# Attention outputs in any of eight PSUM banks, masked products in half-bank pieces on GpSimd, and buffers kept for the open unit

## The chip, the cores and the metric

The kernel runs on one core of a Trainium2 chip. The metric is the device time of one execution in microseconds. The engines of the core are TensorE (PE: matrix products; PEld is its loading of weights), VectorE (DVE), ScalarE (ACT), GpSimd (POOL) and SyncE (SP, which here issues nearly all transfers). PSUM is the memory that TensorE writes; this kernel uses it as eight banks of 128 x 512 float32.

## The reference

One layer mixes an attention block (32 heads of 16, 2048 rows, width 512) with a gated feed-forward network of width 1792:

```python
x = A_x                                            # 1 x 2048 x 512, bf16
g = sigmoid((x * gate_w).sum(-1, keepdims=True))
q, k, v = split(x @ wqkv)                          # 32 heads of 16
p = softmax(einsum("bhqd,bhkd->bhqk", q, k) * 16 ** -0.5)
a = einsum("bhqk,bhkd->bhqd", p, v) @ wo
b = (silu(x @ w_gate) * (x @ w_up)) @ w_down
return g * a + (1 - g) * b
```

The bulk is the softmax: 32 heads x 2048 x 2048 scores, each of which needs an exponential.

## The kernel before

**Units and tiles.** The queries are cut into four blocks of 512 (`QB`), the heads into eight groups of four (`G`). A *unit* is one block and one group, so there are 32. A unit goes over 16 *key tiles* of 128 keys; a key tile has four scores (one per head), each 128 keys x 512 queries, that is one PSUM bank. There are 512 key tiles, 2048 banks of scores.

**Two ways to an exponential.** Most key tiles go to ScalarE: `emit_group` (L913) writes two or three scores side by side as row tiles of TensorE (`score`, L819), and one `Exp` activation reads the banks and writes `e_all` (L255 is the line of every activation, L252 that of every matrix product, L267 that of every instruction of VectorE, GpSimd and SyncE, as helpers record them). The rest, called *masked scores* in this text, go to VectorE: `emit_d` (L1001) lets one or two scores ride in the same row slot, and VectorE turns a bank into 16-bit integers `y` (`c_t`, in one of `NS` = 7 buffers, `take_home`, `home`) whose bits, read as bf16, are a piecewise linear power of two. The curve is mended in one of two ways, chosen per tile by `quad` (L1807):

- a *four-copy tile*: `y` itself and three copies with other integers added (`SHIFTS`) are summed by TensorE, so the tile costs four products with V. Two of the copies are made by VectorE at full width (`copy`, L1104). The third is the *lift*: GpSimd adds the integer (as 32-bit pairs, one bank of `y` is 256 elements) in pieces of one or more banks (`lifted`, L1045).
- a *two-copy tile*: VectorE masks out the mantissa bits and the exponent bits (`bits`, L1113), multiplies `y` by the first mask (`product`, L1122), and TensorE sums product and second mask, two products with V.

**Products with V.** `pv` (L1224) writes four column tiles of 128 x 32 weights that run side by side; over a unit they add up in one bank. That bank is a tile of its own pool, `ps_o`, with one buffer. When a unit is through, `close` (L1647) has VectorE evict the bank (`post`, L1283); `o_ready` (L1654) lets the first product of the next unit start once the eviction is planned to be over. The seven other banks (`NP` = 7, the tile `psum`) go round between scores, masked scores and everything else.

**Side work.** The projections of x to q, k and v, the feed-forward network, the normalisation and the output products are cut into pieces (`columns`, L550) that a `Pacer` releases slot by slot; `side` picks one when TensorE has room before ScalarE's next group is due.

**Order.** The whole order is written out at build time by a planner that keeps estimated clocks for TensorE, VectorE, ScalarE and GpSimd (`plan`), a list of when each bank comes free (`banks`), and constants (L123 to L152) for its choices: how many scores to emit (`choose`, L852), whether another tile goes to VectorE (`v_unit`, L1782), whether it becomes a two-copy tile. `beside` (L1082) puts a lift piece next to reads of PSUM by VectorE, because VectorE's copies from buffer to buffer and GpSimd get in each other's way: a lift waits for the last such copy (`fast_last`), and its size is what fits the reads that follow. Where VectorE has nothing else to do, it makes the rest of the lift itself (`own_now`, L1143).

Each recorded instruction depends on its bank's last user (`ordered`, L217).

Of the kernel before, what the change touches and what calls it, by code (L numbers as in the profile page):

```python
# [80 lines left out]
def kernel(  # L81
# [12 lines left out]
    nc = tc.nc  # L94
# [22 lines left out]
    EB = 9  # L117
    NE = 22
    NP = 7
# [13 lines left out]
    HUNGRY = 0.107  # L133
    KEEP = 2
    FED = 6.808
    W3 = -0.964
    N1 = 6
    N2 = 0.964
    LOW = 1.12
    EXTRA = 1.481  # L140
    NEXT = 1.017
    BURST = 8.876
    SHORT = 17
    BACK = 3
    FIRST = 0.087
    W3T = 0.087
    LATEST = 0.64
# [3 lines left out]
    SPARE = 0.253  # L151

# [12 lines left out]
    ps_o = ctx.enter_context(tc.tile_pool(name="ps_o", bufs=1, space=bass.MemoryType.PSUM))  # L165
# [207 lines left out]
    lift = const.tile([P, 2], U16, name="lift")  # L373
    nc.gpsimd.memset(lift[:], int(SHIFTS[2]))
# [28 lines left out]
    POOL_IN, POOL_FIX, POOL_ONE, POOL_PE, POOL_OVER = 0.12, 0.09, 0.45, 0.2, 0.1  # L403
# [440 lines left out]
    def horizon():  # L844
        return max(plan.act + dur(exps[-1][2]), exps[-1][0] + ACT_IN + ACT_COL * exps[-1][2]) if exps else plan.act
# [6 lines left out]
    def choose():  # L852

        late = max(plan.pe, horizon() - LATEST)
        want = wants()
        fed = thirst()
        side_b = int(side_bank())
        most = min(3, 4 * (hi[au] - at_) - quarter) if au == UNITS - 1 else 3
        hunger = max(0.0, min(1.0, (FED - fed) / FED))

        def left_over(used):
            ok = [b is not None and i not in used for i, b in enumerate(banks)]
            return sum(all(ok[i:i + 3]) for i in range(NP - 2)) + sum(all(ok[i:i + 2]) for i in range(NP - 1))

        def place(w, n, by):
            here = None
            for i, _ in runs(w, by):
                rel = max(banks[i:i + w])
                now = max(late, rel)
                for j, _ in (runs(n, now) if n else [(None, 1)]):  # L870
                    if n and (j < i + w and i < j + n):
                        continue
                    used = [*range(i, i + w), *(range(j, j + n) if n else ())]
                    if n and side_b and not any(b is not None and b <= now and k not in used for k, b in enumerate(banks)):
                        continue
                    got = max([rel] + [banks[k] for k in used])
                    mark = (max(got, plan.pe), -left_over(used), -max(banks[k] for k in used))
                    if here is None or mark < here[0]:
                        here = mark, list(range(i, i + w)), list(range(j, j + n)) if n else [], got
            return here and here[1:]  # L880
        best = None
        for w in range(2, most + 1) if most > 1 else (1,):
            fit = len(fitting(w))
            for n in range(min(want, 2) + 1):
                if n > fit and (fed >= LOW or n > 2):
                    continue
                p = place(w, n, late)
                if p is None:
                    continue
                free = NP - w - sum(b is None for b in banks) - sum(b is not None and b > late for b in banks)  # L890
                value = (W3 + W3T * min(fed, 4.0)) * (w - 2) + hunger * (0.0, N1, N2)[n] - EXTRA * (n > fit) + NEXT * min(free - n, 3)
                if best is None or value > best[0]:
                    best = (value, *p)
        if best:
            return best[1:]
        for w in range(min(2, most), 0, -1):
            p = place(w, 0, 1e9)
            if p:
                return p

    def next_banks(w):

        r, a, t, q = [], au, at_, quarter
        while len(r) < w and a < UNITS:
            r.append(4 * (a * KT + t) + q)
# [7 lines left out]
    def emit_group(s, ds, rel):  # L913
        nonlocal quarter, at_, begun
        w = len(s)
# [8 lines left out]
        e0 = e_run(w)  # L924
        e_next[0] = e0 + w
        k0, step = s[0], s[1] - s[0] if w > 1 else 1
        s_t = psum[:, k0:k0 + (w - 1) * step + 1:step, :]
# [5 lines left out]
        for k, b in enumerate(bs):  # L933
            score(psum[:, s[k], :], b, 32 if riders or w != 2 else 64)
            e_of[b] = e_all[:, e0 + k, :]
            e_slot[b] = e0 + k
# [6 lines left out]
        def exp():  # L943
            act(out=e_all[:, e0:e0 + w, :], in_=s_t, func=ACT.Exp, scale=inv_sqrt_dh)
            plan.act = max(plan.act + ACT_FIX, ready + ACT_IN) + ACT_COL * w
            for i in s:
                banks[i] = plan.act + ACT_PE
            for b in bs:
                e_end[b] = plan.act + ACT_PE
        exps.append((ready, exp, w))  # L950
# [40 lines left out]

    def home(i=None, t=0.0):
# [8 lines left out]
    def emit_d(ks, at_banks, rows=32):  # L1001
        if not vcur:
            n = v_take()
            waiting[n] = [NV, None, take_home()]
            vcur.update(n=n, left=list(range(NV)), y=None)
# [11 lines left out]
        def first():  # L1017
# [8 lines left out]
            if groups[n] == 4 and GPS:  # L1026
                if n not in jobs:
                    jobs[n] = [h, y, None, None, [], 0]
# [4 lines left out]
            if groups[n] == 2:  # L1033
                vops.extend([(0.6, lambda: bits(n, 0, y), ("y", n), n, True), (0.6, lambda: bits(n, 1, y), None, n, True),
                             (MUL_US, lambda: product(n, h, y), None, n, False)])
            else:
                users[h][0] = 2 + GPS
                ready(n, 0, h, y)
                for k in range(1, 4 - GPS):
                    vops.append((0.6, lambda k=k: copy(n, k, h, y), ("y", n) if k == 1 else None, n, True))  # L1040
# [4 lines left out]
    def lifted(n, m=1, own=False):  # L1045

        job = jobs[n]
        h, y, a, c, left, done = job
        if c is None:
            a, t = take_home()  # L1050
            c = job[3] = home(a, 0.0)[1]
# [6 lines left out]
        k = next(i for i in left if all(j in left for j in range(i, i + m)))  # L1058
        cols = slice(k * QBW, (k + m) * QBW)
        if own:  # L1060
            spend_v(0.07 + 0.1335 * m, 0.0, None, True)
            vec.tensor_scalar(out=c[:, cols], in0=y[:, cols], scalar1=SHIFTS[2], scalar2=None, op0=ALU.add)
            fast_last[0] = last_of[vec.engine.engine]
        else:
            ins = gps.tensor_tensor(out=c[:, cols].bitcast(I32), in0=y[:, cols].bitcast(I32),
                                    in1=lift[:, :].bitcast(I32).broadcast_to([P, m * QBW // 2]), op=ALU.add)
# [8 lines left out]
        if job[5] == NV:  # L1075
            jobs.pop(n)
            copies[n, 3] = (c.bitcast(BF16), a)
            vready.append((end, n, 3))
            drop(h, end)
            y_live[0] -= 1  # L1080

    def beside(span):  # L1082

        if not jobs or plan.pool > plan.dve + 0.05:
            return
        n = next(iter(jobs))
        left = sorted(jobs[n][4])
        if not left or jobs[n][3] is None and min(c_free) > plan.dve:
            return
# [14 lines left out]
    def copy(n, k, i, y):  # L1104
        h, c = home()
        vec.tensor_scalar(out=c, in0=y, scalar1=SHIFTS[k - 1], scalar2=None, op0=ALU.add)
        ready(n, k, h, c)
        if k == 3 - GPS:
            drop(i, plan.dve + 0.05)
            if not GPS:  # L1110
                y_live[0] -= 1

    def bits(n, k, y):  # L1113
        h, c = home()
# [14 lines left out]
    def c_ready():  # L1129
        return min(c_free) if not vops or vops[0][4] else 0.0  # L1130
# [6 lines left out]
    def pay_v():  # L1137
        cost, f, key, _, _ = vops.pop(0)
# [4 lines left out]
    def own_now(now):  # L1143

        if not jobs:
            return False
        n = next(iter(jobs))
        left = sorted(jobs[n][4])
        if not left or len(left) + jobs[n][5] < NV or jobs[n][3] is None and min(c_free) > now:
# [74 lines left out]
    def pv(n, k=None, most=QBW):  # L1224
# [12 lines left out]
        o = o_of[un]  # L1237
        first = pvs[un] in ((0, KT // 2) if un == 0 else (0,))
# [44 lines left out]
    def post(un):  # L1283
        qb, g = UNIT[un]
        osbs[un] = osb0[qb] if g == 0 else work.tile([P, QBW], BF16, tag="osb", name="osb")
        if un == 0:
            assert part_scaled
            vec.scalar_tensor_tensor(out=osbs[un][:, :], in0=o_of.pop(un)[:, :], scalar=tiny[:, 0:1], in1=o_part, op0=ALU.add, op1=ALU.add)
        elif un == UNITS - 1:
            act(out=osbs[un][:, :], in_=o_of.pop(un)[:, :], func=ACT.Identity, bias=tiny[:, 0:1], scale=1.0)  # L1290
        else:
            vec.tensor_scalar(out=osbs[un][:, :], in0=o_of.pop(un)[:, :], scalar1=tiny[:, 0:1], scalar2=None, op0=ALU.add)
# [79 lines left out]
    def tail(n):  # L1372

        for _ in range(n):
            tq, i = rest.pop(0)
            if tq == 3 and i == 0:
                a_ps.append(ps_o.tile([P, QBW], F32, tag="o", name="al_o"))
# [21 lines left out]
    warm = ps_o.tile([P, QBW], F32, tag="o", name="warm")  # L1399
# [56 lines left out]
    m_free(qp0, plan.pe + 2.0)  # L1456
    for g in (3, 4):
# [196 lines left out]
    def o_ready(now):  # L1654
        return closed in o_of or now is None or not closed or closed - 1 in osbs and o_end[0] <= now
# [35 lines left out]
    def begin(n):  # L1691
        plan.slot = n
        for c in need.get(n, []):
# [54 lines left out]
    def next_pv():  # L1748
        flush_act()
        while not pv_list(None):  # L1750
# [6 lines left out]
            elif jobs and jobs[next(iter(jobs))][4]:  # L1757
                lifted(next(iter(jobs)))
# [23 lines left out]
    def v_unit():  # L1782

        nonlocal vu
        if y_live[0] >= NY or min(c_free) >= 1e9 or sum(v[0] for v in vops) > 4.9 or (au, at_) < (0, 2):
# [186 lines left out]
```

## Time and profile before

| | us |
|---|---|
| median of 3 runs (763.38 to 765.28) | 763.42 |
| the profiled execution, its own time | 765.53 |
| its span, first to last instruction | 763.8 |
| PE busy / DVE busy | 744.7 / 718.6 |
| ACT busy / POOL busy | 744.6 / 192.3 |

Of the groups of instructions these matter as well: products with V in the row `o_ps<-e_all,vaug` (2012 instructions, 167.2 us) and `o_ps<-c_t,vaug` (1864, 142.0), scores in `psum<-qx,kaug` (1632, 253.7), the tanh of the gate in `th<-psum` (56, 34.4), the eviction of a unit's output in `osb<-o_ps,tiny` (30, 22.3, mean 744 ns).

How to read it: busy time counts a moment once per engine, however many instructions overlap in it, so four column tiles of 385 ns that run side by side count little more than one. A row gives how many instructions there are, their busy time, the mean of one, then the idle time of the engine just before them and what ended it. The chain of waits follows back from the last instruction to what released each one. In the view by stage each row is a stretch of the span with the busy time of every engine, the granted clock of TensorE, and the share and rate of the transfers.

### The profile page before, as it was taken

The numbers are of one execution on the slowest core, as the hardware profiler recorded it, in microseconds if no ns is written. First come the engines' busy times: TensorE is split into PE (matmuls) and PEld (weight loads), VectorE is DVE, ScalarE is ACT, GpSimd is POOL, SyncE is SP. The second block draws the span as 40 slices with busy tenths as digits, with TensorE's granted clock in tenths as the row PEclk, the third lists the DMA queues.
The fourth block names the chain that finished last, engine by engine and source line by source line (L and its number), as shares of the span: only waits on it lengthen the run. The fifth ranks groups of instructions, "written<-read, shape, count | busy, mean of one in ns | idle before, by whom it ended". The sixth has DMA issues, their size and how long they took to land.

```text
span 763.8 us, 24745 instructions
## 1 busy us (share of the span) xinstructions
PE 744.7 (98%) x10201; PEld 241.6 (32%) x10201; DVE 718.6 (94%) x1190; ACT 744.6 (97%) x835; POOL 192.3 (25%) x312
## 2 busy tenths in 40 slices
PE   8999999999999998999999999999999999999997
PEld 3333333333233332333233333333333333333232
DVE  6799999999999999899999999999999999999994
ACT  5999999999999999999999999999999999999996
POOL 5231120120433013334321113334212034131130
PEclk9999999999999999999999999999999999999999
DMA  9000212254210013121200041311000232100001
GB/s 220 10 2 15 50 33 47 52 135 89 62 28 10 17 44 77 31 62 30 50 13 18 23 103 35 76 34 44 8 23 19 68 79 45 44 19 12 15 30 36
DMA packets 91033, 34.57 MB, mean 45 GB/s; under 512 B 75488, under 2 KB 90472, under 8 KB 90920
## 3 DMA queue, kind: packets, MB, share of 16 engines
q1 hardware_dynamic: 89192, 32.66, 18.1%
q8 instruction: 80, 1.31, 0.7%
q10 hardware_dynamic: 1728, 0.33, 0.2%
q14 instruction: 33, 0.27, 0.1%
HBM read 21.55 MB, written 2.35 MB: 31 GB/s over the span
## 4 chain that ended last, share of the span: by engine, by line
PE 51%; ACT 29%; DVE 13%; issue 6%; DMA 1%; DVEq 0%; ACTq 0%
PE psum L252 34%; ACT e_all L255 27%; PE o_ps L252 16%; DVE c_t L267 7%; DVE kaug L267 2%; DVE mt L267 1%; DVE gs L267 1%; ACT th L255 1%; PE warm L252 1%; DVE osb L267 0%; DMA wg<-in_B_w_gate_dram 0%; DVE rd L267 0%; DMA out_dram<-o_t 0%; DVE o_t L267 0%; PE al_o L252 0%
## 5 line engine op out<-in xcount | busy, mean ns | idle before, releaser
L255 ACT ACTIVATE e_all<-psum 128x1024 bf16<-128x1024 f32 x766 | 716.7, 1044 | 4.0 <-PE psum L252 2.4
L267 DVE TENSOR_SCALAR c_t<-psum 128x512 uint16<-128x512 f32 x440 | 292.6, 683 | 16.3 <-PE psum L252 14.8
L252 PE MATMUL psum<-qx,kaug 32*128 32x512 bf16 (+1 forms) x1632 | 253.7, 385 | 8.1 <-ACT e_all L255 5.2
L267 POOL TENSOR_TENSOR c_t<-c_t,lift 128x256 int32<-128x256 int32 (+2 forms) x218 | 137.7, 637 | 427.2 <-DVE c_t L267 337.3
L252 PE MATMUL o_ps<-e_all,vaug 128*32 128x512 bf16 (+3 forms) x2012 | 167.2, 333 | 0.0
L252 PEld LDWEIGHTS <-kaug 32*128 32x128 bf16 (+1 forms) x2048 | 76.4, 91 | 273.1 <-ACT e_all L255 188.2
L252 PE MATMUL o_ps<-c_t,vaug 128*32 128x512 bf16 (+3 forms) x1864 | 142.0, 337 | 0.4 <-DVE osb L267 0.4
L252 PEld LDWEIGHTS <-vaug 128*32 128x32 bf16 x4204 | 102.0, 95 | 124.8 <-issue 88.8
L267 DVE TENSOR_SCALAR c_t<-c_t 128x2048 uint16<-128x2048 uint16 (+2 forms) x188 | 127.0, 683 | 1.6
L252 PE MATMUL psum<-wd_t,mt 128*32 128x512 bf16 x896 | 75.1, 382 | 0.0
L252 PE MATMUL psum<-xT,wg 128*32 128x512 bf16 x896 | 72.2, 384 | 0.1
L252 PE MATMUL psum<-xT,wu 128*32 128x512 bf16 x896 | 71.5, 383 | 0.4 <-DVE c_t L267 0.2
L252 PE MATMUL psum<-q,kaug 32*128 32x512 bf16 (+1 forms) x256 | 50.0, 385 | 0.5 <-ACT e_all L255 0.2
L267 DVE TENSOR_SCALAR kaug<-psum 128x512 uint16<-128x512 f32 x72 | 47.9, 683 | 2.1 <-PE psum L252 1.8
L252 PE MATMUL psum<-xT,wqk 128*32 128x512 bf16 x512 | 41.8, 384 | 0.2 <-DVE c_t L267 0.2
L267 DVE TENSOR_TENSOR c_t<-c_t 128x2048 bf16<-128x2048 bf16 x34 | 41.5, 1220 | 0.0
L267 DVE SCALAR_TENSOR_TENSOR mt<-gs,psum 128x512 bf16<-128x512 bf16 x56 | 38.2, 682 | 2.8 <-PE psum L252 0.3
L267 DVE SCALAR_TENSOR_TENSOR gs<-th,psum 128x512 bf16<-128x512 bf16 x56 | 38.1, 679 | 1.7 <-ACT th L255 1.4
L267 POOL TENSOR_TENSOR c_t<-kaug,lift 128x256 int32<-128x256 int32 (+1 forms) x36 | 23.4, 654 | 60.8 <-DVE c_t L267 35.7
L255 ACT ACTIVATE th<-psum 128x512 bf16<-128x512 f32 x56 | 34.4, 615 | 0.0
L267 POOL TENSOR_TENSOR kaug<-c_t,lift 128x256 int32<-128x256 int32 (+1 forms) x28 | 18.4, 660 | 61.4 <-DVE c_t L267 54.6
L252 PEld LDWEIGHTS <-mt 128*32 128x32 bf16 (+1 forms) x1037 | 24.1, 95 | 28.6 <-issue 21.7
(125 smaller groups left out, 411.5 us busy)
## 6 DMA issues: line engine op xcount, KB each, us to landing
wg<-in_B_w_gate_dram SPq DMA_DIRECT2D x56, 128.0 KB
wu<-in_B_w_up_dram SPq DMA_DIRECT2D x56, 128.0 KB
on<-osb SPq DMA_DIRECT2D x120, 16.0 KB
rb<-rr SPq DMA_DIRECT2D x15, 128.0 KB
wd_t<-in_B_w_down_dram SPq DMA_DIRECT2D x7, 256.0 KB
qx<-qst SPq DMA_DIRECT2D x96, 16.0 KB
qx<-aq SPq DMA_DIRECT2D x96, 16.0 KB
out_dram<-o_t SPq DMA_DIRECT2D x12, 128.0 KB
```

The lines of the kernel that those rows point to most:

```text
L252: return ordered(nc.tensor.matmul(out, lhsT=lhsT, rhs=rhs, **kw), [lhsT, rhs], [out])
L255: ordered(nc.scalar.activation(out=out, in_=in_, **kw), [in_, *kw.values()], [out])
L267: return ordered(f(*a, **kw), [v for v in (*a, *kw.values()) if v is not out], [out])
```

## The change

Three things and a new set of constants.

1. The pool `ps_o` is gone. The eight banks are one tile (`NP` = 8), and a unit's output takes whichever bank is free (`m_tile("o")`); `o_ready` asks for a free bank and no longer for the old output's eviction.
2. `take_over` lets GpSimd have the product of a two-copy tile: when `beside` finds no lift piece to do, it takes the first masked product that is waiting (`TAKE_P`), in up to eight pieces of half a bank (256 columns of bf16, `width`), if the planned time is enough before its unit ends (`GLEAD`, `WINDOW`). VectorE makes a rest of it itself, as with lifts. The same function can take a copy of a four-copy tile (`TAKE_C`), which stays off in all sets of constants.
3. `home_at` keeps one buffer back for the unit that is being summed: a later unit is given the second free one, as long as the open unit still `needs` buffers.

Besides, `choose` can emit two pairs of scores at once (`place_two`), `horizon` adds up all waiting exponentials, `EB` becomes 8, and `begin` switches all of the planner's constants at slots 24, 240, 384, 456 and 480 (`WEIGHTS`).

```diff
-    EB = 9
+    EB = 8
-    NP = 7
+    NP = 8
-    ps_o = ctx.enter_context(tc.tile_pool(name="ps_o", bufs=1, space=bass.MemoryType.PSUM))
...
-    POOL_IN, POOL_FIX, POOL_ONE, POOL_PE, POOL_OVER = 0.12, 0.09, 0.45, 0.2, 0.1
+    POOL_IN, POOL_FIX, POOL_ONE, POOL_PE, POOL_OVER = 0.12, 0.12, 0.43, 0.2, 0.1
+    TAKE_P = 1
...
+    def home_at(n):
+
+        short = n // KT > closed and any(v > 0 and m // KT == closed for m, v in needs.items())
+        return sorted(c_free)[1 if short else 0]
...
     def lifted(n, m=1, own=False):
 
-        job = jobs[n]
-        h, y, a, c, left, done = job
+        h, y, a, c, left, done, kind = job = jobs[n]
...
+        width, every = (QBW // 2, 2 * NV) if kind == "P" else (QBW, NV)
+        k = next((i for i in left if all(j in left for j in range(i, i + m))))
+        cols = slice(k * width, (k + m) * width)
...
+            if kind == "P":
+                ins = gps.tensor_tensor(out=c.bitcast(BF16)[:, cols], in0=y.bitcast(BF16)[:, cols], in1=c.bitcast(BF16)[:, cols], op=ALU.mult)
+            else:
+                ins = gps.tensor_tensor(out=c[:, cols].bitcast(I32), in0=y[:, cols].bitcast(I32),
+                                        in1=lift[:, kind, :].bitcast(I32).broadcast_to([P, m * QBW // 2]), op=ALU.add)
...
+    def take_over():
+
+        seen = set()
+        for i, (_, _, _, n, _, what) in enumerate(vops):
+            first = n not in seen
+            seen.add(n)
+            if what is None or n // KT < au:
+                continue
+            if what[0] == "P" and TAKE_P and first and n not in jobs and plan.dve + 2 * NV * WINDOW + GLEAD <= until(n):
+                _, h, y = what
+                a, c = part.pop(n)
+                vops.pop(i)
+                jobs[n] = [h, y, a, c, list(range(2 * NV)), 0, "P"]
+                return n
...
     def beside(span):
 
-        if not jobs or plan.pool > plan.dve + 0.05:
+        if plan.pool > plan.dve + 0.05:
             return
-        n = next(iter(jobs))
+        n = workable(plan.dve)
+        if n is None:
+            n = take_over()
+            if n is None or n != workable(plan.dve):
+                return
...
         if un not in o_of:
-            while un and un - 1 not in osbs:
-                pay()
-            plan.pe = max(plan.pe, o_end[0])
-            o_of[un] = ps_o.tile([P, QBW], F32, tag="o", name="o_ps")
+            o_of[un] = m_tile("o")
...
     def o_ready(now):
-        return closed in o_of or now is None or not closed or closed - 1 in osbs and o_end[0] <= now
+        if closed in o_of or now is None:
+            return True
+        t = m_ready()
+        return t is not None and t <= now
...
     def begin(n):
         plan.slot = n
+        if n in WEIGHTS:
+            HUNGRY, KEEP, FED, W3, W3T, W4, W4T, W4B, N1, N2, LOW, EXTRA, NEXT, SPARE, BURST, SHORT, BACK, FIRST, EB, OWN, NY, TAKE_C, TAKE_P, GLEAD, WINDOW, FACE = WEIGHTS[n]
```

More of the change, by code (lines that the diff above doesn't have):

```diff
@@ L132 @@
     D_US = (0.0, 0.6, 1.133)
-    HUNGRY = 0.107
+    HUNGRY = 0
     KEEP = 2
[L135 to L143, printed above, removed]
+    FED = 5.957
+    W3 = -0.349
+    N1 = 6.622
+    N2 = 1.455
+    LOW = 1.05
+    EXTRA = 2.223
+    NEXT = 0.999
+    BURST = 8.931
+    SHORT = 18
     BACK = 3
-    FIRST = 0.087
+    FIRST = 0.059
     W3T = 0.087
+    W4 = -1
+    W4T = 0.1
+    W4B = 0.1
     LATEST = 0.64
@@ L371 @@
         nc.gpsimd.memset(sel_t[32 * j:32 * j + 1, j:j + 1], 1.0)
-    lift = const.tile([P, 2], U16, name="lift")
-    nc.gpsimd.memset(lift[:], int(SHIFTS[2]))
+    lift = const.tile([P, 3, 2], U16, name="lift")
+    for i in range(3):
+        nc.gpsimd.memset(lift[:, i, :], int(SHIFTS[i]))
     kb = const.tile([P, NB], F32, name="kb")
@@ L880, in place, with place_two @@
             return here and here[1:]
-        best = None
+        def place_two(n, by):
+            here = None
+            two = [i for i, _ in runs(2, by)]
+            for i in two:
+                for i2 in two:
+                    if i2 < i + 2:
+                        continue
+                    first = [i, i + 1, i2, i2 + 1]
+                    rel = max(banks[k] for k in first)
+                    for j, _ in (runs(n, max(late, rel)) if n else [(None, 1)]):
+                        more = list(range(j, j + n)) if n else []
+                        if any(k in first for k in more):
+                            continue
+                        used = first + more
+                        if side_b and not any(b is not None and b <= by and k not in used for k, b in enumerate(banks)):
+                            continue
+                        got = max(banks[k] for k in used)
+                        mark = (max(got, plan.pe), -left_over(used), -max(banks[k] for k in used))
+                        if here is None or mark < here[0]:
+                            here = mark, [[i, i + 1], [i2, i2 + 1]], more, got
+            return here and here[1:]
+        best = None
+        left = (hi[au] - at_) * 4 - quarter
+        if left >= 4 and len(e_slot) // 2 + 2 <= EB and e_run(4) is not None and not exps:
+            for n in range(min(want, 2) + 1):
+                if n and fed >= LOW:
+                    continue
+                p = place_two(n, late)
+                if p is None:
+                    continue
+                free = NP - 4 - sum(b is None for b in banks) - sum(b is not None and b > late for b in banks)
+                value = W4 + W4T * min(fed, 4.0) + W4B * min(len(pv_list(None)), 5) + hunger * (0.0, N1, N2)[n] - EXTRA * (n > 0) + NEXT * min(free - n, 3)
+                if best is None or value > best[0]:
+                    best = (value, *p)
         for w in range(2, most + 1) if most > 1 else (1,):
@@ L898, in choose, with face @@
             if p:
-                return p
+                return ([p[0]], *p[1:])
+    facing = {}
+    def face():
+        forward()
+        if FACE and quarter == 0 and au < UNITS:
+            n = au * KT + at_
+            facing.pop(n, None)
+            plain = len(fitting(2))
+            facing[n] = 2
+            if len(fitting(2)) <= plain:
+                facing.pop(n)
     def next_banks(w):
@@ L934, in emit_group @@
             score(psum[:, s[k], :], b, 32 if riders or w != 2 else 64)
-            e_of[b] = e_all[:, e0 + k, :]
-            e_slot[b] = e0 + k
+        done = 0
+        todo = []
+        for p in parts_:
+            e0 = e_run(len(p))
+            e_next[0] = e0 + len(p)
+            for k, b in enumerate(bs[done:done + len(p)]):
+                e_of[b] = e_all[:, e0 + k, :]
+                e_slot[b] = e0 + k
+            todo.append((p, bs[done:done + len(p)], e0))
+            done += len(p)
         if riders:
@@ L941, in emit_group, with exp @@
         ready = start + TO_ACT
[L943 to L950, printed above, removed]
+        for p, pb, e0 in todo:
+            def exp(p=p, pb=pb, e0=e0, w=len(p)):
+                act(out=e_all[:, e0:e0 + w, :], in_=psum[:, p[0]:p[0] + w, :], func=ACT.Exp, scale=inv_sqrt_dh)
+                plan.act = max(plan.act + ACT_FIX, ready + ACT_IN) + ACT_COL * w
+                for i in p:
+                    banks[i] = plan.act + ACT_PE
+                for b in pb:
+                    e_end[b] = plan.act + ACT_PE
+            exps.append((ready, exp, len(p)))
         for _ in bs:
@@ L1057, in lifted @@
         left.sort()
-        k = next(i for i in left if all(j in left for j in range(i, i + m)))
-        cols = slice(k * QBW, (k + m) * QBW)
+        width, every = (QBW // 2, 2 * NV) if kind == "P" else (QBW, NV)
+        k = next((i for i in left if all(j in left for j in range(i, i + m))))
+        cols = slice(k * width, (k + m) * width)
         if own:
-            spend_v(0.07 + 0.1335 * m, 0.0, None, True)
-            vec.tensor_scalar(out=c[:, cols], in0=y[:, cols], scalar1=SHIFTS[2], scalar2=None, op0=ALU.add)
+            spend_v(0.07 + (0.133 if kind == "P" else 0.1335) * m, 0.0, None, True)
+            if kind == "P":
+                vec.tensor_tensor(out=c.bitcast(BF16)[:, cols], in0=y.bitcast(BF16)[:, cols], in1=c.bitcast(BF16)[:, cols], op=ALU.mult)
+            else:
+                vec.tensor_scalar(out=c[:, cols], in0=y[:, cols], scalar1=SHIFTS[kind], scalar2=None, op0=ALU.add)
             fast_last[0] = last_of[vec.engine.engine]
         else:
-            ins = gps.tensor_tensor(out=c[:, cols].bitcast(I32), in0=y[:, cols].bitcast(I32),
-                                    in1=lift[:, :].bitcast(I32).broadcast_to([P, m * QBW // 2]), op=ALU.add)
+            if kind == "P":
+                ins = gps.tensor_tensor(out=c.bitcast(BF16)[:, cols], in0=y.bitcast(BF16)[:, cols], in1=c.bitcast(BF16)[:, cols], op=ALU.mult)
+            else:
+                ins = gps.tensor_tensor(out=c[:, cols].bitcast(I32), in0=y[:, cols].bitcast(I32),
+                                        in1=lift[:, kind, :].bitcast(I32).broadcast_to([P, m * QBW // 2]), op=ALU.add)
             if fast_last[0] is not None:
@@ L1074, in lifted @@
         job[5] = done + m
-        if job[5] == NV:
+        if job[5] == every:
             jobs.pop(n)
-            copies[n, 3] = (c.bitcast(BF16), a)
-            vready.append((end, n, 3))
-            drop(h, end)
-            y_live[0] -= 1
+            more = taken.pop(n, None)
+            if kind == "P":
+                copies[n, 1] = (c.bitcast(BF16), a)
+                vready.append((end, n, 1))
+            else:
+                copies[n, kind + 1] = (c.bitcast(BF16), a)
+                vready.append((end, n, kind + 1))
+            drop(h, end)
+            if more is None:
+                y_live[0] -= 1
+            else:
+                jobs[n] = more
@@ new lines, with until @@
+    taken = {}
+    def until(n):
+        un = n // KT
+        return plan.act + (hi[au] - at_) * TILE_US + (hi[un] * TILE_US if un > au else 0.0)
+    def take_over():
[4 more added lines that the diff above has]
+            if what is None or n // KT < au:
+                continue
+            if what[0] == "P" and TAKE_P and first and n not in jobs and plan.dve + 2 * NV * WINDOW + GLEAD <= until(n):
[4 more added lines that the diff above has]
+                return n
+            if what[0] == "C" and TAKE_C and what[1] == 2 and plan.dve + (NV + (len(jobs[n][4]) if n in jobs else 0)) * WINDOW + GLEAD <= until(n) and home_at(n) <= plan.dve:
+                _, k, h, y = what
+                vops.pop(i)
+                more = [h, y, None, None, list(range(NV)), 0, k - 1]
+                if n in jobs:
+                    taken[n] = more
+                else:
+                    jobs[n] = more
+                    y_live[0] += 1
+                return n
+        return None
@@ L1082, in beside, with workable @@
+    def workable(now):
+        for n, job in jobs.items():
+            if job[4] and (job[3] is not None or home_at(n) <= now):
+                return n
+        return None
     def beside(span):
-        if not jobs or plan.pool > plan.dve + 0.05:
+        if plan.pool > plan.dve + 0.05:
             return
-        n = next(iter(jobs))
+        n = workable(plan.dve)
[3 more added lines that the diff above has]
+                return
@@ L1107, in copy @@
         ready(n, k, h, c)
[L1108 to L1111, printed above, removed]
+        drop(i, plan.dve + 0.05)
     def bits(n, k, y):
+        needs[n] -= 1
         h, c = home()
@@ L1137, in pay_v @@
     def pay_v():
-        cost, f, key, _, _ = vops.pop(0)
+        cost, f, key = vops.pop(0)[:3]
         spend_v(cost, 0.0, key, True)
@@ L1143, in own_now @@
     def own_now(now):
-        if not jobs:
+        n = workable(now)
+        if n is None:
             return False
-        n = next(iter(jobs))
         left = sorted(jobs[n][4])
-        if not left or len(left) + jobs[n][5] < NV or jobs[n][3] is None and min(c_free) > now:
+        if len(left) + jobs[n][5] < (2 * NV if jobs[n][6] == "P" else NV):
             return False
@@ L1376, in tail @@
             if tq == 3 and i == 0:
[L1377 removed]
+                a_ps.append(m_tile("al_o"))
             w, r = last_rows(tq)(i)
@@ L1398 @@
     qp0 = take(4)
-    warm = ps_o.tile([P, QBW], F32, tag="o", name="warm")
+    warm = take(7)
     def keep_warm(n):
@@ L1756, in next_pv @@
                 pay()
-            elif jobs and jobs[next(iter(jobs))][4]:
-                lifted(next(iter(jobs)))
+            elif workable(1e8) is not None:
+                lifted(workable(1e8))
             else:
@@ L1784, in v_unit @@
         nonlocal vu
-        if y_live[0] >= NY or min(c_free) >= 1e9 or sum(v[0] for v in vops) > 4.9 or (au, at_) < (0, 2):
+        if y_live[0] >= NY or home_at(max(vu, au) * KT) >= 1e9 or sum(v[0] for v in vops) > 4.9 or (au, at_) < (0, 2):
             return None
```

54 lines of the change are left out of this document (34 added, 20 removed).

## The prediction

> **What bounds the kernel now.** I read the page's head first, then the busy time by stage, then the groups by shape, then the chain of waits, and last the timeline around a few places.
>
> ```profile
> PE 744.7 (98%) x10201; PEld 241.6 (32%) x10201; DVE 718.6 (94%) x1190; ACT 744.6 (97%) x835; POOL 192.3 (25%) x312
> ...
> PE 51%; ACT 29%; DVE 13%; issue 6%; DMA 1%; DVEq 0%; ACTq 0%
> ```
>
> Three engines are nearly full and the chain changes between them all the time: a balanced pipeline, in which less work on one engine helps only as far as the two others let it. GpSimd (POOL) is three quarters idle. By stage (PE, PEld, DVE, ACT, POOL busy, granted clock, DMA share, GB/s), from the first full stretch to the last exponentials:
>
> ```profile
> 30.00:750.00 720.00, 709.05 (x9848) 228.07 (x9846) 694.23 (x1130) 717.22 (x804) 179.84 (x283) 1.00 0.17 41
> ```
>
> ScalarE is idle for 2.8 of 720 us. Its rows, and those of VectorE and GpSimd, by shape:
>
> ```profile
> L255 ACT ACTIVATE e_all<-psum 128x1024 bf16<-128x1024 f32 x766 | 716.7, 1044 | 4.0 <-PE psum L252 2.4 <-PE o_ps L252 0.2 <-ACT e_all L255 0.2
> L267 DVE TENSOR_SCALAR c_t<-psum 128x512 uint16<-128x512 f32 x440 | 292.6, 683 | 16.3 <-PE psum L252 14.8
> L267 POOL TENSOR_TENSOR c_t<-c_t,lift 128x256 int32<-128x256 int32 x207 | 126.0, 613 | 418.4 <-DVE c_t L267 330.0 <-PE psum L252 31.3 <-DVE kaug L267 24.2
> L267 DVE TENSOR_SCALAR c_t<-c_t 128x2048 uint16<-128x2048 uint16 x184 | 125.7, 690 | 1.4
> ...
> L267 DVE TENSOR_TENSOR c_t<-c_t 128x2048 bf16<-128x2048 bf16 x34 | 41.5, 1220 | 0.0
> ```
>
> An exponential lasts 1044 ns, but they overlap: in the timeline the closest starts lie 904 ns apart, and half of the 745 in this stretch lie within 921. The mean is 929. From the first at 13.8 us to 752 the intervals hold 20.6 us above 904 ns (478 ns behind a tanh): 7.4 us are jitter under 40 ns each, 13.2 us are 111 real stalls. TensorE, counted by slots (four column tiles or two to four row tiles that run side by side), starts a 512-column slot 0.217 us after one of its own kind and 0.32 us after one of the other kind; with that price it has about 17 us left over in the 720. VectorE has 26. **ScalarE sets the pace**, with TensorE and VectorE about 2.5% and 3.5% behind.
>
> One stall in this profile is foreign. Rows of the timeline, ScalarE alone (start, duration, what it was idle for):
>
> ```profile
> 302.34 2.92 ACT L255 ACTIVATE e_all<-psum 128x1024 bf16<-128x1024 f32 x3
> 305.80 1.02 ACT L255 ACTIVATE e_all<-psum 128x1024 bf16<-128x1024 f32 x1 [0.53 <-PE psum L252]
> 307.42 1.02 ACT L255 ACTIVATE e_all<-psum 128x1024 bf16<-128x1024 f32 x1 [0.60 <-PE psum L252]
> ```
>
> and the stage around it:
>
> ```profile
> 305.00:307.00 2.00, 2.00 (x25) 0.52 (x17) 0.00 (x0) 1.29 (x2) 0.61 (x1) 0.50 0.14 33
> ```
>
> The granted clock is 0.50 there, and three intervals of ScalarE are 745, 721 and 119 ns too long, 1.6 us together. The profiled execution took 765.53 (span 763.8 and 1.7 around it); without that stall it is 763.9, and the median of the runs is 763.42. I make the sums against this execution and put the difference on 763.42.
>
> **The change part by part.** The counts are from the order of instructions of both kernels, the durations from the rows above.
>
> *ScalarE.* 766 pair exponentials become 759 pairs and 2 triples, that is 1532 banks become 1524: two more key tiles go to VectorE (129 to 131). A pair costs 904 ns and a tanh on one bank 478, so a bank is 0.426 and a triple 1.330. 766 x 0.904 = 692.5; 759 x 0.904 + 2 x 1.330 = 688.8. **Minus 3.7 us**, on the engine that sets the pace. The 56 tanhs stay.
>
> *VectorE.* Evictions of masked scores 516 to 524, +8 x 0.683 = +5.5. Two-copy tiles (two masks and a product) 48 to 55, four-copy tiles 81 to 76; whole-tile copies and masks 261 to 262, +0.7; left-over pieces that it lifts itself +1.2 at most (an estimate, by width from the 0.690 row). Whole products 48 to 38 and two partial ones (1792 and 1024 columns): -10 x 1.22 + 1.8 = -10.4. Sum **-3.0 us**.
>
> *TensorE.* Products of e or c with V fall by 8 full slots (two-copy for four-copy tiles), score slots rise by 6 (more lone masked scores), changes of kind rise by 3 and cut slots by 10 (each start 13 ns late): -2 x 0.217 + 3 x 0.107 + 10 x 0.013 = **0.0 us**. So TensorE keeps its load while ScalarE loses 3.7 of its own: TensorE's reserve in the main stretch falls from 17 to about 13 us.
>
> *GpSimd.* Lift pieces 286 to 257, and 87 new product pieces (125 units of 256 columns, 15.6 tiles). No row shows a product on GpSimd. Below, I take a lift's time for it: both move 256 elements per unit, 0.612 for one, 1.039 for two (0.427 per unit). It could be faster only if the second operand, a real stream here and a repeated word in a lift, were free; nothing speaks for that. Above, VectorE's rows give a product 1220 to a copy's 690, 1.77 times, so a unit would be 0.755 and a piece 0.94. I take 0.612, the same engine's row. Then lifts go from 183 to 171 us and products add 70: busy 192 to about 250 of 760, hidden as to GpSimd itself. SyncE issues 584 transfers in both. The cover of a piece is the PSUM read beside which it is put, and what it costs without cover stands in the timeline:
>
> ```profile
> 303.80 0.61 POOL L267 TENSOR_TENSOR c_t<-c_t,lift 128x256 int32<-128x256 int32 x1 [1.38 <-DVE c_t L267]
> ...
> 304.24 0.73 DVE L267 TENSOR_SCALAR c_t<-c_t 128x2048 uint16<-128x2048 uint16 x1
> ```
>
> The copy began 0.17 us before the piece ended, and took 0.73 for 0.685. Over all 54 such overlaps the copy or product on VectorE is longer by what the overlap has over 0.136 us: it stands still until GpSimd is done; PSUM reads are not touched (683 with and without). Before, 117 of 286 pieces have no more PSUM reads behind them than units; after, 98 of 257 lifts and 25 of 87 products (38 units). At 0.612 the overlaps cost what they cost now. At 0.94 those 38 units cost 38 x 0.33 = 12.5 us of VectorE. [...]
>
> *Attention output in any bank.* The next unit's first product no longer waits until VectorE has read the old output. At the 31 turnovers the products with V pause 1.9 us (median, start to start), but TensorE fills it with scores and FFN slots: its idle time put down to the output's eviction is 0.4 us in all, and ScalarE's stalls within 0.9 us before to 2 us after the evictions sum to 1.9. Bounds: 0 to -1.9 us; against it stands that at a turnover two banks hold outputs and six are left for scores, where seven were. I take 0.
>
> *Buffers kept for the open unit, and the planner's new constants.* They decide the order and are in the counts above; what they do to the 11.6 us of stalls that are left without the foreign one no row shows. Bounds: half of them gone, -5.8, or half as many again, +5.8. I take 0, since the same three engines stay within 3% of each other.
>
> Sum: -3.7 + 0 + 0: 763.42 - 3.7 = 759.7, and with some of the saved time lost because TensorE did not get lighter (0.2 of the 4 us it gives up) **759.9**.
>
> **Rivals.** *TensorE takes over the pace* (no change). For: its load is the same to 0.1 us and it leads the chain with 51%. Against: it has 17 us left in 720, and much of its idle time is put down to ScalarE's exponentials. The saving becomes stalls of ScalarE waiting for scores: 763.4 less a quarter of 3.7, 762.5. *Stalls shrink as well*: the turnovers' 1.9 and a third of the other 9.7 go, 759.7 - 5.1 = 754.6. *Products on GpSimd run long* (slower). Mechanism: a piece that outlasts its PSUM read holds VectorE's next copy, and so the eviction behind it, the free banks and the next scores. It decides from a unit of about 0.70 us on, where 38 x 0.27 = 10.3 less 3.0 is a third of VectorE's 26 us reserve; at 0.755 VectorE gains 9.5 us instead of losing 3. Taking two thirds on the path, 6.3, 759.7 + 6.3 = 766.0, and 767 with late products at the ends of units.
>
> **How the numbers follow.** Forecast 0.50; TensorE takes over 0.20; stalls shrink too 0.12; long products 0.18. A measurement of this kernel tells 0.3% (2.3 us) from no change, so faster is under 761.1 and slower over 765.7: faster 0.62, same 0.22 (with a part of the long products), slower 0.16. The range leaves out most of the two outer cases' far ends: 756.0 to 766.0.
>
> **What would show it.** Right: 761 exponentials still 904 to 930 ns apart, product pieces near 0.61 us, whole VectorE products 38 at 1.22, TensorE's idle time down by about 4 us in the main stretch. Wrong: intervals of ScalarE over 40 ns late summing to 15 us or more with scores as releaser (TensorE's case); product pieces of 0.7 us or more and VectorE copies near 0.8 (the slow case); POOL waits that end on late masks, and products with V missing at a unit's end.

## The result, and the profile after

| | before | changed |
|---|---|---|
| median of the runs, us | 763.4 (763.33 to 765.28) | **772.9** (772.11 to 773.79) |
| profiled execution, its own time / span | 765.53 / 763.8 | 773.47 / 771.7 |

The ratio is 1.0119, 95% interval 1.0098 to 1.0139: 1.2% slower, where 0.5% faster was forecast. The runs of the kernel before lie in two groups, 763.0 to 763.4 and 764.7 to 765.5; its profile belongs to the second and shows a stretch at half clock (the foreign stall of the prediction).

The head of the page of the changed kernel, with one line of its slices (a fortieth of the span, 19.3 us, per digit):

```profile
PE 744.7 (96%) x10241; PEld 241.9 (31%) x10241; DVE 719.3 (93%) x1192; ACT 741.3 (96%) x830; POOL 255.7 (33%) x372
...
ACT  5999999769999999999999999999999999999996
...
PE 63%; ACT 25%; DVE 5%; issue 4%; SPq 1%; DMA 1%; ACTq 0%; DVEq 0%
...
L259 ACT ACTIVATE e_all<-psum 128x1024 bf16<-128x1024 f32 x761 | 713.0, 1045 | 16.1 <-PE psum L256 15.0
```

The busy times moved little: ScalarE 3.3 us less, TensorE the same, GpSimd 256 where about 250 was expected, and VectorE 0.7 more where 3.0 less was summed. The 9.5 us did not come from any of them. The row of the exponentials tells where to look: idle before them rose from 4.0 to 16.1 us. The slices show it in two places of forty, and the waits (who waited for what: us in total, times, longest) put a name to it:

```profile
ACT e_all L259 <- PE psum L256: 15.0, 9, 10.8
...
PE psum L256 <- DMA wd_t<-in_B_w_down_dram: 10.2, 1, 10.2
```

One wait of TensorE, once, for a transfer. The timeline of TensorE and then of SyncE's queue around it (start, duration):

```profile
147.46 0.39 PE L256 MATMUL psum<-c_t,vaug 128*32 128x512 bf16 x4
147.82 0.39 PE L256 MATMUL psum<-qx,kaug 64*128 64x512 bf16 x2
158.44 0.62 PE L256 MATMUL psum<-wd_t,vaug 128*32 128x512 bf16 x4 [10.24 <-DMA wd_t<-in_B_w_down_dram]
```

```profile
144.11 4.94 SPq L271 DMA_DIRECT2D qx<-qst  x8
149.15 0.53 SPq L271 DMA_DIRECT2D wg<-in_B_w_gate_dram  x1
149.77 0.45 SPq L271 DMA_DIRECT2D wu<-in_B_w_up_dram  x1
150.31 4.93 SPq L271 DMA_DIRECT2D qx<-aq  x8
155.35 0.53 SPq L271 DMA_DIRECT2D wd_t<-in_B_w_down_dram  x1
```

GpSimd's rows just before (start, duration):

```profile
144.83 1.79 POOL L271 TENSOR_TENSOR wd_t<-c_t,wd_t 128x256 bf16<-128x256 bf16 x2 [1.10 <-DVE c_t L271]
147.51 0.67 POOL L271 TENSOR_TENSOR wd_t<-c_t,wd_t 128x256 bf16<-128x256 bf16 x1 [0.90 <-DVE c_t L271]
```

The matrix product at 158.44 is a product with V (`<-wd_t,vaug`) whose operand lies in the seventh of the buffers for masked scores. `home` (L992 before) puts that buffer inside `wd_t`, the place kept for w_down, until w_down is loaded. `begin` gives out the loads by slot number alone, the first at slot 88. In the changed kernel this tile's mask is ready at 132.7 us, and GpSimd makes the product with it in seven pieces from 134.7 to 148.2 us, so that the product with V comes later in the order than the load. It therefore waits for the load, and the load waits its turn behind 18 transfers that SyncE issues at about 0.6 us each. Two of the four banks then hold w_down instead of the product. In the kernel before, the same buffer has seen its last product with V some 24 us before the load is issued (how often; duration in ns, shortest, median, longest; first and last start):

```profile
L252 PE MATMUL o_ps<-wd_t,vaug x60: 216/273/393, 46.3 to 127.7; 128*32 128x128 bf16 x28, 128*32 128x512 bf16 x12, 128*32 128x384 bf16 x12, 128*32 128x256 bf16 x8
L267 SPq DMA_DIRECT2D wd_t<-in_B_w_down_dram x7: 457/500/1360, 152.4 to 183.5; - x7
```

TensorE's clock is lowered as well, from the middle of the wait on (each row a stretch: PE, PEld, DVE, ACT and POOL busy, granted clock, DMA share, GB/s):

```profile
158.00:160.00 2.00, 1.55 (x14) 0.41 (x14) 0.00 (x0) 0.00 (x0) 0.00 (x0) 0.50 0.44 98
160.00:162.00 2.00, 2.00 (x25) 0.61 (x27) 0.06 (x1) 1.06 (x2) 0.00 (x0) 0.50 0.41 131
```

The granted clock is 0.50 from 153.2, five microseconds after the last matrix product, to 163.5, five microseconds after the next. ScalarE's intervals are 10.94 us too long across the wait, and 0.71 and 0.76 at half clock behind it: 12.4 us in all.

### The profile page after: what moved, and what is told of

Read it like the earlier page. It is cut to its first block, busy times and chain, and to the rows that moved or that the text cites. A ratio compares the mean times of both kernels' runs of the same rounds, so it can differ in the third digit from the quotient of the medians.

```text
span 771.7 us, 24939 instructions
## 1 busy us (share of the span) xinstructions
PE 744.7 (96%) x10241; PEld 241.9 (31%) x10241; DVE 719.3 (93%) x1192; ACT 741.3 (96%) x830; POOL 255.7 (33%) x372
## 4 chain that ended last, share of the span: by engine, by line
PE 63%; ACT 25%; DVE 5%; issue 4%; SPq 1%; DMA 1%; ACTq 0%; DVEq 0%
PE psum L256 63%; ACT e_all L259 24%; DVE c_t L271 4%; SPq L271 1%; DVE mt L271 1%; ACT th L259 1%; DVE gs L271 0%; DMA wd_t<-in_B_w_down_dram 0%; ACT mt L259 0%; DMA on<-osb 0%; ACT xT L259 0%; DVE aq L271 0%; ACT osb L259 0%; DVE osb L271 0%; DVE mt L321 0%
## 5 line engine op out<-in xcount | busy, mean ns | idle before, releaser
L259 ACT ACTIVATE e_all<-psum 128x1024 bf16<-128x1024 f32 x761 | 713.0, 1045 | 16.1 <-PE psum L256 15.0
L271 DVE TENSOR_SCALAR c_t<-psum 128x512 uint16<-128x512 f32 x444 | 296.0, 683 | 23.3 <-PE psum L256 21.7
L271 POOL TENSOR_TENSOR c_t<-c_t,lift 128x256 int32<-128x256 int32 (+1 forms) x184 | 122.2, 668 | 301.6 <-DVE c_t L271 251.9
L256 PE MATMUL psum<-e_all,vaug 128*32 128x512 bf16 (+3 forms) x2092 | 174.7, 327 | 0.0
L256 PE MATMUL psum<-c_t,vaug 128*32 128x512 bf16 (+3 forms) x1856 | 142.3, 335 | 0.4 <-DVE c_t L271 0.2
L271 DVE TENSOR_SCALAR c_t<-c_t 128x2048 uint16<-128x2048 uint16 (+1 forms) x192 | 130.5, 688 | 1.1
L271 POOL TENSOR_TENSOR c_t<-c_t 128x256 bf16<-128x256 bf16 (+3 forms) x59 | 51.5, 884 | 77.0 <-DVE c_t L271 63.4
L256 PE MATMUL psum<-xT,wg 128*32 128x512 bf16 x896 | 75.2, 388 | 0.4 <-DVE gs L271 0.3
L271 DVE TENSOR_SCALAR kaug<-psum 128x512 uint16<-128x512 f32 x68 | 45.3, 683 | 1.9 <-PE psum L256 1.8
L271 POOL TENSOR_TENSOR kaug<-c_t,lift 128x256 int32<-128x256 int32 (+1 forms) x31 | 20.1, 654 | 44.1 <-DVE c_t L271 37.5
```

Source lines behind the costliest of these rows:

```text
L256: return ordered(nc.tensor.matmul(out, lhsT=lhsT, rhs=rhs, **kw), [lhsT, rhs], [out])
L259: ordered(nc.scalar.activation(out=out, in_=in_, **kw), [in_, *kw.values()], [out])
L271: return ordered(f(*a, **kw), [v for v in (*a, *kw.values()) if v is not out], [out])
```

## Experiments

Nine kernels. "Closest starts" is ScalarE's work as in the prediction: pairs x 0.904 + triples x 1.330.

**1. The loads 8 slots later.** The order of instructions on TensorE, VectorE, ScalarE and GpSimd is the same as in the changed kernel.

```diff
-        i = n - (QB + 1) * KT - 8
+        i = n - (QB + 1) * KT - 16
```

> The changed kernel with the seven loads of w_down given out 8 slots later, so that the first of them stands behind the products that still read the buffer inside wd_t; counts of instructions on every engine stay as in the changed kernel. Theory A (the loss is the one wait of TensorE for that load, 10.9 us of ScalarE, and 0.7 + 0.8 us at half clock behind it): 772.9 - 12.4 = 760.5, between 759.5 and 761.5, and no interval of ScalarE of more than 2 us. Rival B (the loss is spread: GpSimd's product pieces, now 0.67 us for one and 1.15 for two, hold VectorE): 771 to 774.

Measured: **761.25** us (760.5 to 762.14, 9 runs), ratio to the kernel before 0.9964 (0.9952 to 0.9976). The chain and the exponentials:

```profile
PE 63%; ACT 27%; issue 5%; DVE 4%; DMA 1%; ACTq 0%; DVEq 0%
```

```profile
L259 ACT ACTIVATE e_all<-psum 128x1024 bf16<-128x1024 f32 x761 | 712.7, 1044 | 4.1 <-PE psum L256 3.0 <-ACT e_all L259 0.3
```

Idle before the exponentials is back at 4.1 us, and the longest interval is 1.1 us over. Theory A holds: 11.7 us came back, 12.4 were expected. Rival B does not: GpSimd's pieces are the same and as long here.

**2. The load at its old place in the order, from another queue.**

```diff
-        queue.dma_start(out=wd_t[:, f:f + 2, :], ...
+        (gps if f == 0 else queue).dma_start(out=wd_t[:, f:f + 2, :], ...
```

> The changed kernel with only the first load of w_down issued from GpSimd's queue instead of SyncE's, at the same place of the order: it still stands ahead of the products with V that read the buffer, but no longer behind the 18 transfers that SyncE issues from 144.1 to 155.3 us. Theory A with the queue as its price: the load starts near 148.2 us and lands some 3 to 4 us later, the stall falls from 10.2 to 3 to 4 us and the clock stays up or dips less: 763 to 766. Rival (the transfer or its buffer is slow, not the queue): the stall stays near 10 us and the time at 772.

Measured: 762.98 us (762.14 to 764.42), ratio 0.999 (0.9977 to 1.0004). GpSimd's queue and TensorE:

```profile
146.09 0.95 POOL L271 DMA_DIRECT2D wd_t<-in_B_w_down_dram  x1
147.06 0.68 POOL L271 TENSOR_TENSOR wd_t<-c_t,wd_t 128x256 bf16<-128x256 bf16 x1
```

```profile
147.35 0.39 PE L256 MATMUL psum<-qx,kaug 64*128 64x512 bf16 x2
149.44 0.40 PE L256 MATMUL psum<-wd_t,vaug 128*32 128x512 bf16 x4 [1.70 <-DMA wd_t<-in_B_w_down_dram]
```

The load stands ahead of the last piece of the product, so the crossing is in the order itself. It lands 3.3 us after its issue, much as it does from SyncE (155.35 to 158.40, 3.1 us), but it is issued some 9 us earlier. The wait is 1.7 us, less than expected, and the clock stays at 1.00. So of the 10.2 us some 8.5 are SyncE's queue, and the rest is the transfer itself.

**3. Such a crossing put into the kernel before**, by giving out its loads 16 slots earlier. This leaves out the order between the last uses of the buffer and the load: a lift of VectorE overwrites what the load brought, and products with V read it.

```diff
-        i = n - (QB + 1) * KT - 8
+        i = n - (QB + 1) * KT + 8
```

> The kernel before, with the seven loads of w_down given out 16 slots earlier, so that the first stands ahead of twelve cut products with V (and one left-over lift of VectorE) that use the buffer inside wd_t; these then read or overwrite what the load brought. All else is as before. Theory A (a product that comes behind the load in the order waits until SyncE has issued it and it has landed): TensorE idles once, put down to the load, for 2 to 8 us, and the time is 765 to 772. Rival (such a crossing costs nothing as long as the load itself is quick): 763.

Measured: 763.96 us (763.29 to 765.58), ratio 0.9998 (0.9986 to 1.001). The expectation of 2 to 8 us fails. The crossing is there:

```profile
DVE wd_t L267 <- DMA wd_t<-in_B_w_down_dram: 1.1, 1, 1.1
PEld L252 <- DMA wd_t<-in_B_w_down_dram: 0.6, 1, 0.6
```

but SyncE issues the load at 121.99, some 2 us before VectorE would begin the lift, so that the lift and the products behind it stand still for 1.1 us only. With the second run: being behind the load costs little; what costs is when the load's turn comes.

**4. No products on GpSimd** (loads late from here on; they stay on VectorE).

```diff
-    TAKE_P = 1
+    TAKE_P = 0
...
+    WEIGHTS = {k: v[:22] + (0,) + v[23:] for k, v in WEIGHTS.items()}
```

> The late loads of the first run, and no products on GpSimd: the planner then gives VectorE 127 key tiles instead of 131, and ScalarE 761 pairs and 6 triples, 1540 banks instead of 1524. If the products bring what the counts say: 761 x 0.904 + 6 x 1.330 = 695.9 against 688.8, so 7 us over the first run, about 767.5. If the long pieces cost VectorE as much as they save: within 1.5 us of the first run.

Measured: 767.48 us, 6.2 over the first run: the products are worth what the counts say.

**5. The old rule for a unit's output.**

```diff
-        t = m_ready()
-        return t is not None and t <= now
+        return closed in o_of or now is None or not closed or closed - 1 in osbs and o_end[0] <= now
...
+            while un and un - 1 not in osbs:
+                pay()
+            plan.pe = max(plan.pe, o_end[0])
             o_of[un] = m_tile("o")
```

> The late loads of the first run, and the old rule for a unit's output: the next unit's first product with V waits until the old output has been evicted, though it may take any of the eight banks. ScalarE then has 755 pairs, 7 triples and one single, 692.3 us by the closest starts, 3.5 more than in the first run. If the free choice of the bank is worth what the counts say: 764. If its worth is only the turnovers' 0.4 us of TensorE that the prediction named: 761.

Measured: 764.69 us, 3.4 over the first run. By the counts its worth is not the 0.4 us of idle TensorE; it is two key tiles (129 on VectorE instead of 131) that the planner can no longer place.

**6. No kept buffer.**

```diff
-        return sorted(c_free)[1 if short else 0]
+        return sorted(c_free)[0]
```

> The late loads of the first run, and no buffer kept back for the open unit (the first free one is given to any unit). ScalarE has 758 pairs and 4 triples, 690.5 us by the closest starts against 688.8. If the time follows ScalarE's work: 761.25 + 1.7 = 763. If the kept buffer saves late products at the ends of units, more stalls come on top: 764 or more. If it does nothing: 761.

Measured: 762.1 us (761.42 to 762.31), 0.9 over the first run, whose own runs reach from 760.5 to 762.14. That is less than the 1.7 of the counts and within the scatter; its worth is small, and this run cannot size it.

**7. One set of constants** (`WEIGHTS = {}`).

> The late loads of the first run, and one set of planner's constants for the whole run instead of five. ScalarE has 768 pairs, 694.3 us against 688.8. If the time follows ScalarE's work: 761.25 + 5.5 = 766.7. If the sets matter only by the stalls they avoid and not by the counts: 761 to 763.

Measured: 767.46 us, near the 766.7 of ScalarE's work: the five sets are worth their counts.

**8. The constants of the kernel before** (`WEIGHTS = {}`, and thirteen of those that the diff changes set back; the planner's estimates of GpSimd's times stay as changed).

> The late loads of the first run, with the eight free banks, the products on GpSimd and the kept buffer, but the planner's constants of the kernel before. ScalarE has 768 pairs (766 before), GpSimd 49 units of products (125 in the changed kernel). If the time follows ScalarE's work: 694.3 against 692.5 before, 763.3 + 1.8 = 765, or 766.7 counted from the first run. If the new freedom itself is the gain and the constants are beside the point: 761 to 762.

Measured: 767.54 us, ratio to the kernel before 1.0039 (1.0026 to 1.0053). The freedom alone, planned with the old constants, is slower than the kernel before.

**9. The planner told GpSimd's true times.**

```diff
-            plan.pool = max(plan.pool, plan.dve + POOL_IN) + POOL_FIX + POOL_ONE * m
+            plan.pool = max(plan.pool, plan.dve + POOL_IN) + (0.185 + 0.485 * m if kind == "P" else 0.185 + 0.427 * m)
```

> The late loads of the first run, with the planner told what GpSimd's pieces take in the traces (0.185 + 0.485 per unit for a product, 0.185 + 0.427 for a lift, instead of 0.12 + 0.43 for both). It then hands over 68 units of products instead of 125, and ScalarE has 759 pairs and 6 triples, 694.1 us. If the time follows ScalarE's work: 761.25 + 5.3 = 766.5. If the mis-stated times cost VectorE stalls that now go: 760 to 763.

Measured: 765.29 us, 4.0 over the first run. A truer estimate moved work back to ScalarE, with the constants left as they were.

Together, ScalarE's work by closest starts against the time:

| kernel | closest starts, us | median, us |
|---|---|---|
| changed, loads late (1) | 688.8 | 761.25 |
| no kept buffer (6) | 690.5 | 762.1 |
| old output rule (5) | 692.3 | 764.69 |
| before | 692.5 | 763.26 |
| true GpSimd times (9) | 694.1 | 765.29 |
| one set (7) | 694.3 | 767.46 |
| old constants (8) | 694.3 | 767.54 |
| no products (4) | 695.9 | 767.48 |

Seven microseconds of ScalarE's work span 6.3 of time, and no kernel is off that line by more than about 1.5 us. The row of the kernel before has its median beside runs 1, 2, 4 and 5; beside runs 6 to 9 it was 765.08. The first run of the list beats both kernels.

## Why the prediction was wrong

**The step that failed** is the part on GpSimd: "hidden as to GpSimd itself. SyncE issues 584 transfers in both." The transfers were counted (582 in both traces, not 584), not placed. A product that takes up to eight pieces beside PSUM reads ends much later than one instruction of VectorE, so its product with V moved past a transfer that reuses the buffer. The text followed what a late piece does to VectorE's next copy, and did not ask what else is given out by slot number and uses the same memory. The cost of 12.4 us appears in no term and no rival. "Late products at the ends of units" was the nearest, priced at 1 us. Of the 13.0 us by which the forecast of 759.9 is missed, 11.7 went when the crossing was taken out (run 1, 761.25).

Whether a plan crosses depends on which tile gets that buffer last. Where GpSimd makes a product in it late (the changed kernel, runs 1, 2, 6 and 7), TensorE's last product with V from it starts at 147.5 us or later. Where it does not (runs 4, 5, 8 and 9), that is over by 143 us, ahead of the 146 us at which GpSimd's order reached the load in run 2. These runs have the late loads, so that they would not have crossed at the old slot is read from their traces and was not tried.

**What bounds the kernel.** Right. With the crossing gone, the time follows ScalarE's work over eight kernels. From run 1 to run 4 ScalarE is busy 6.9 us longer (741.0 to 747.9) and the time grows by 6.2, while TensorE (741.6 and 741.3) and VectorE (719.2 and 719.1) are as busy as before.

**ScalarE, minus 3.7.** Right: 761 exponentials, closest starts 903 to 904 ns. From the kernel before to the first experiment the medians fall by 2.0 and the lowest runs by 2.5 (762.98 to 760.5).

**VectorE, minus 3.0, and the products' price.** The counts hold, as they come from the order itself; the unit price was too low. GpSimd's rows in the changed kernel:

```profile
L271 POOL TENSOR_TENSOR c_t<-c_t,lift 128x256 int32<-128x256 int32 x161 | 98.8, 616 | 280.9 <-DVE c_t L271 236.6 <-DVE kaug L271 25.4 <-PE psum L256 9.0
L271 POOL TENSOR_TENSOR c_t<-c_t 128x256 bf16<-128x256 bf16 x38 | 25.4, 671 | 58.1 <-DVE c_t L271 48.4 <-DVE kaug L271 6.6 <-DVE aq L271 3.1
...
L271 POOL TENSOR_TENSOR c_t<-c_t 128x512 bf16<-128x512 bf16 x17 | 19.5, 1154 | 13.4 <-DVE c_t L271 11.6 <-DVE kaug L271 1.8
```

A unit of a product is 0.485 us (1.154 - 0.671) on 0.186, where the lift's 0.427 was taken and 0.755 was the upper bound. What it costs is small: in the first experiment 21 products overlap a copy or product of VectorE and lengthen them by 1.2 us in all, and lifts by 2.2 (2.0 before). That is 1.4 of the 3.7 us by which VectorE's busy time misses the sum; the rest was not followed up. With VectorE busy 95% of the time and GpSimd 34% (run 1), handing the products over paid: experiment 4 puts the move's worth at 6 us.

**TensorE, 0.0.** Right: its busy time is 741.6 us in the first experiment and 742.2 in run 3, which has the order of the kernel before and no stretch at half clock on the way. Its idle time from 30 to 745 us falls from 11.7 us (run 3) to 9.0, by 2.7 and not by about 4. The chain now goes by it for 63% instead of 51%, but the sign named for its taking over the pace is not there: ScalarE's intervals that are over 40 ns late sum to 12.3 us in the first experiment, not to 15 or more.

**Attention output in any bank, taken at 0 with bounds to -1.9.** Too low, and asked in the wrong way. The worth was looked for in idle time at the turnovers; it lies in the tiles that the planner places, 3.4 us in experiment 5, and was already in the counts. So the part-by-part sum booked it under ScalarE.

**Rivals.** Long products: mechanism seen, price a tenth of what the rival needs. Stalls shrink: no; without the crossing the intervals hold 20.8 us over the closest starts, against 20.6 before, of which 1.6 were foreign. That is 1.8 us more, about the size of the rest between 759.9 and 761.25. Two stalls of the first experiment are new. One of 1.1 us ends at 33.3 us, where a forced piece of side work and sixteen gate products stand ahead of the next scores; it is in every kernel made from the changed one but the one with the old constants. One of 1.0 us ends at 695.5 us and is in the changed kernel and in runs 2 and 6 as well. The cause of neither was tried, and it stays open.

## What to carry to other kernels

When a piece of work gets slower but hidden, list everything that is ordered by count or by slot and shares its memory, and look at which side of each it now falls: a sum of busy times does not show a crossing. A load given out ahead of the last reader of its buffer costs what is left of its queue and its transfer, here 1 us, 1.7 us or 10 us. Where a planner balances three engines, price a change by the work that the bounding engine loses after the plan is made, since even an edit that saves no idle time (the free output bank) pays by the tiles it lets the planner move.

## What the runs showed of the hardware

- In the kernel before, 54 copies and products of VectorE between buffers at full width (2048 columns) overlapped a GpSimd instruction; 53 of them were longer by the overlap beyond 0.136 us, to within 11 ns, and one was shorter. VectorE's reads of PSUM were not (683 ns with and without). GpSimd was held up as well: seven of its pieces of 256 elements that began over 0.136 us before the end of a narrower VectorE instruction between buffers took 650 to 727 ns instead of 612.
- SyncE issued the eight small transfers of a `qx` group at 0.62 us each, so 18 transfers held a load for about 11 us; from GpSimd's queue the same load was issued and landed within 3.4 us (146.09 to 149.44).
- TensorE was granted half its clock for 3.4 us from 304.1 us of the kernel before, which cost ScalarE 1.6 us; its longest idle stretches in the 20 us ahead were of 0.53 us (busy 1.98 of the 3 us up to 303). In the changed kernel it stood still for 10.2 us and had half its clock for 10.2 us, half of them while idle; in run 2 it stood still for 1.7 us and the clock stayed at 1.00.
